# Strassen's seven products for the down projection of a fused attention and SwiGLU kernel, with casts moved from GpSimd to ScalarE

## The chip, the cores and the metric

The kernel runs on one core of a Trainium2 chip. The metric is the device time of one execution in microseconds. Before the change it took 389.86 us (median of 3 runs, 389.35 to 390.61). A run counts as slow when it takes over 1.5% longer than the fastest of the same kernel.

A word on names. PE is TensorE, DVE is VectorE, ACT is ScalarE, POOL is GpSimd, SP is SyncE. L634 is line 634 of that kernel's own source; the same statement has another line number in another kernel.

## The reference

Selective attention over 8 batches of 8 heads (sequence 576, head dimension 64), then a SwiGLU feed-forward block over all 4608 tokens, each with 512 features:

```python
scores = q @ k.T / sqrt(64)              # causal, plus min(bias, 0) from a cumulated s
attn   = exp(scores - max); attn /= attn.sum() + 1e-9
x      = (attn @ v) as (4608, 512)
g      = x @ w_gate                      # (512, 1536)
out    = (silu(g) * (x @ w_val)) @ w_out # w_out is (1536, 512), the "down projection"
```

Inputs and output are fp32; the kernel computes in bf16 with fp32 accumulation.

## The kernel before

After a start-up of about 32 us, in which batch 0 is attended, the kernel goes through nine **token tiles** of 512 tokens, numbered 0 to 8. Each has a **gate/value stage** (12 feature blocks of 128; for each a gate group and a value group of four 512-wide matmuls) and a **down stage** (four row groups of twelve 512-wide matmuls). The attention of the later batches is woven between the groups of tiles 0 to 5 and the start of tile 6: a generator yields after each group and the attention is pumped up to a given position. Every engine works through its own list in the order in which the program issues it. Eight PSUM banks are handed round by `take` and `give`.

```python
def ffn_items(tt):
    xt = XT[:, :, (tt % 3) * TT : (tt % 3 + 1) * TT]
    hts = []
    # ... the stores left over from the tile before are issued here
    for ft in range(NFT):                       # 12 feature blocks
        gbs = take(); pg = view(gbs, TT)
        for c in range(4):
            nc.tensor.matmul(pg, WG[j][:, c, f0:f0+128], xt[:, c, :], start=(c==0), stop=(c==3))
        nc.scalar.activation(th, pg, AF.Tanh, scale=0.5)
        nc.vector.scalar_tensor_tensor(pp, in0=th, scalar=1.0, in1=pg, op0=ALU.add, op1=ALU.mult)
        give(gbs)
        yield 1
        vbs = take(); pv = view(vbs, TT)
        # ... four matmuls with WV into pv
        ht = hpool.tile([128, TT], BF16, tag="ht", bufs=16, name="ht")
        nc.vector.tensor_mul(ht, pp, pv)
        give(vbs)
        hts.append(ht)
        yield 1
    for ts_ in range(4):                        # the down stage
        ybs = take(); py = view(ybs, DM)
        for ft in range(NFT):
            nc.tensor.matmul(py, hts[ft][:, ts_*128:(ts_+1)*128], WO[ft//WKO][:, ft%WKO, :],
                             start=(ft == 0), stop=(ft == NFT - 1))
            if ft % 4 == 3 and ft < NFT - 1:
                yield 1
        ysb = yp.tile([128, DM], FP32, tag="y", name="ysb")
        nc.scalar.mul(ysb, py, 0.5)
        give(ybs)
        # ... the store of the row group before is issued on GpSimd's queue
        yield 1
    # (the last row group of tile 8 goes in two halves of 256 columns, stored by SP)
```

What the attention does for the half-batch (four heads) that comes next stands beside this. SP loads fp32 keys and queries, they are cast to bf16 (`ck`, `cq`), written to memory (`ks`, `qs`), read back transposed (`pk`, `pq`), and copied by VectorE into the two halves of `kq`, from which PE takes the scores. GpSimd also casts the values (`rawv` to `vt`), masks the exponentials (`affine_select`), and issues the store of each finished pair of heads (`ot` to `xs`), which SP reads back transposed into `XT`.

```python
def side(h, step):                              # h: half-batch, step: head within it
    # ...
        if step == 0: transposes(h + 1); aug(h + 1, GP4)
        if step == 2: split(h + 1, "k", nc.vector)    # 2 copies pk -> kq, 64x1152 bf16
        if step == 3: split(h + 1, "q", nc.vector)    # 2 copies pq -> kq
    # ...
        if step == 1: cast_one(h + 2, "k", nc.gpsimd)
        if step == 2: cast_one(h + 2, "q", nc.gpsimd)
        if step == 3: scratch(h + 2)
    # ...  on odd h, V of the next batch: five casts on GpSimd, in steps 1, 2 and 3
```

The softmax here doesn't subtract the row's maximum and nothing guards it: scores larger than these inputs give would overflow.

## Time and profile before

| | before |
|---|---|
| time, median | 389.86 us |
| span in the profile | 388.6 us |
| PE busy | 371.3 us, 96% |
| tiles 2 to 5, each, first gate matmul to next tile's first | 40.4, 40.2, 40.2, 40.3 us |
| of which gate/value and down | 26.9 to 27.1 and 13.3 us |
| tiles 6, 7, 8 | 36.4, 31.8, 31.3 us |
| last matmul to end of span | 4.2 us |

The tile times are read off the timeline: where the first matmul with `wg` of a tile starts, and the first one with `wo`. As PE hardly stops in the middle of the kernel, they add up to the span. The end in the timeline (start, duration, engine, line, operation, output and inputs, count, and in brackets the idle time before it with what ended it):

```profile
382.80 1.58 PE L604 MATMUL bank<-wo,ht 128*128 128x256 bf16 x13
...
383.52 1.69 SPq L614 DMA_DIRECT2D out_dram<-yh  x2
384.42 0.42 DVE L613 TENSOR_SCALAR yh<-bank 128x256 f32<-128x256 f32 x1 [9.15 <-PE bank L604]
```

After PE's last matmul only one eviction of 256 columns and one small store remain.

### The profile page before, as it was taken

How to read it: one execution, taken by the hardware profiler on the slowest of the kernel's cores; microseconds unless marked ns; L12 is line 12 of the kernel's file. 1: busy time of each engine (PE TensorE's matmuls, PEld its weight loads, DVE VectorE, ACT ScalarE, POOL GpSimd, SP SyncE). 2: the span in 40 equal slices, each digit the busy share in tenths (PEclk: the TensorE clock that was granted, in tenths of full speed). 3: DMA queues.
4: the chain of work that ended last, by engine and by line, in shares of the span. 5: the costliest groups of instructions: out<-in, count | busy, mean ns of one | idle time of the engine just before them, and what ended most of it. 6: DMA issues, size and time to landing. Idle time of an engine off the chain costs nothing.

```text
span 388.6 us, 7949 instructions
## 1 busy us (share of the span) xinstructions
PE 371.3 (96%) x3006; PEld 206.2 (53%) x3006; DVE 239.8 (62%) x431; ACT 214.5 (55%) x411; POOL 192.3 (49%) x329
## 2 busy tenths in 40 slices
PE   3779999999999999999999999999999999999995
PEld 3565556655555555555555555555555544444443
DVE  7676777468653786369735884488347625733750
ACT  7686877567646565566556655565464513323321
POOL 7683368656695756566656666576342220011001
PEclk9999999999999999999999999999999999999999
DMA  7999999996859998996789757964231222002002
GB/s 245 196 244 261 197 264 257 303 254 165 158 153 269 287 221 220 211 267 153 184 215 288 122 178 142 293 159 98 61 113 35 32 73 69 3 27 81 2 12 97
DMA packets 100534, 64.18 MB, mean 165 GB/s; under 512 B 81888, under 2 KB 85824, under 8 KB 100496
## 3 DMA queue, kind: packets, MB, share of 16 engines
q1 hardware_dynamic: 90816, 45.36, 50.3%
q0 software_dynamic: 9680, 18.32, 18.2%
q8 instruction: 23, 0.38, 0.4%
q14 instruction: 15, 0.12, 0.1%
HBM read 37.90 MB, written 19.86 MB: 149 GB/s over the span
## 4 chain that ended last, share of the span: by engine, by line
PE 82%; DVE 6%; DMA 5%; issue 3%; ACT 2%; POOL 0%; DVEq 0%; ACTq 0%; SPq 0%; POOLq 0%
PE bank L571 21%; PE bank L620 21%; PE bank L586 20%; PE bank L367 9%; PE bank L405 6%; DMA pk<-ks 2%; PE wide L367 2%; DVE pp L578 2%; ACT pt L380 1%; DVE ht L591 1%; DVE kq L320 1%; DMA kq<-HL 1%; PE one L405 1%; DMA XT<-xs 1%; DMA s_sb<-in_s_dram 1%
## 5 line engine op out<-in xcount | busy, mean ns | idle before, releaser
L380 ACT ACTIVATE pt<-bank 128x512 bf16<-128x512 f32 x224 | 104.1, 504 | 40.3 <-PE bank L367 28.5
L578 DVE SCALAR_TENSOR_TENSOR pp<-th,bank 128x512 bf16<-128x512 bf16 x108 | 74.1, 686 | 69.8 <-ACT th L576 69.0
L571 PE MATMUL bank<-XT,wg 128*128 128x512 bf16 x432 | 111.0, 379 | 1.1 <-DMA XT<-xs 0.5
L586 PE MATMUL bank<-XT,wv 128*128 128x512 bf16 x432 | 110.9, 379 | 0.2 <-DVE pp L578 0.2
L576 ACT ACTIVATE th<-bank 128x512 bf16<-128x512 f32 x108 | 64.5, 597 | 78.2 <-PE bank L571 73.9
L620 PE MATMUL bank<-wo,ht 128*128 128x512 bf16 x420 | 102.4, 379 | 0.0
L591 DVE TENSOR_TENSOR ht<-pp,bank 128x512 bf16<-128x512 bf16 x108 | 74.0, 685 | 8.8
L367 PEld LDWEIGHTS <-kq 128*128 128x128 bf16 x576 | 46.5, 99 | 40.3 <-issue 6.1
L367 PE MATMUL bank<-kq 128*128 128x128 bf16 (+4 forms) x504 | 65.9, 240 | 0.7 <-DVE ht L591 0.5
L383 POOL TENSOR_SCALAR_AFFINE_SELECT pt<-pt 128x512 bf16<-128x512 bf16 x64 | 41.0, 640 | 34.3 <-ACT pt L380 33.7
L571 PEld LDWEIGHTS <-wg 128*128 128x128 bf16 x432 | 38.3, 98 | 36.6 <-issue 1.2
L586 PEld LDWEIGHTS <-wv 128*128 128x128 bf16 x432 | 38.4, 98 | 35.1 <-issue 1.1
L620 PEld LDWEIGHTS <-ht 128*128 128x128 bf16 x420 | 37.1, 98 | 34.4
L405 PEld LDWEIGHTS <-pt 128*128 128x128 bf16 x960 | 41.5, 98 | 20.7
L439 POOL DMA_DIRECT2D xs<-ot x24 | 21.9, 913 | 60.8 <-DVE ot L422 60.8
L634 POOL DMA_DIRECT2D out_dram<-ysb x35 | 19.7, 562 | 60.9 <-ACT ysb L628 60.9
L628 ACT ACTIVATE ysb<-bank 128x512 f32<-128x512 f32 x35 | 20.9, 597 | 40.9 <-PE bank L620 39.7
L405 PE MATMUL bank<-vt,pt 128*128 128x65 bf16 x840 | 42.8, 194 | 0.0
L190 POOL DMA_DIRECT2D kq<-HL x52 | 31.3, 602 | 2.0 <-PE bank L571 1.6
L421 DVE RECIPROCAL rc<-bank 128x5 f32<-128x5 f32 x56 | 10.6, 190 | 34.4 <-PE bank L405 34.4
L422 DVE TENSOR_TENSOR ot<-bank,rc 128x320 bf16<-128x320 f32 x56 | 27.5, 491 | 1.9
L388 POOL TENSOR_SCALAR_AFFINE_SELECT pt<-pt 128x64 bf16<-128x64 bf16 x64 | 16.4, 256 | 21.3 <-ACT pt L380 21.1
(68 smaller groups left out, 211.1 us busy)
## 6 DMA issues: line engine op xcount, KB each, us to landing
out_dram<-ysb POOLq DMA_DIRECT2D x35, 256.0 KB, 3.3
rawk<-in_k_dram SPq DMA_DIRECT2D x15, 576.0 KB
rawq<-in_q_dram SPq DMA_DIRECT2D x15, 576.0 KB
rawv<-in_v_dram SPq DMA_DIRECT2D x32, 256.0 KB
xs<-ot POOLq DMA_DIRECT2D x24, 160.0 KB, 3.9
ks<-ck SPq DMA_DIRECT2D x11, 288.0 KB
qs<-cq SPq DMA_DIRECT2D x11, 288.0 KB
wg<-in_moe_w_gate_dram POOLq DMA_DIRECT2D x2, 768.0 KB, 11.6
```

What stands on the lines that cost most here:

```text
L190: engs[hh].dma_start(KQ[hb % 2][r][r0 : r0 + 4, :, e * S : (e + 1) * S], HL[bh : bh + 1, :, :, :],)
L367: nc.tensor.matmul(sc[:, o : o + w], T[:, 1, e * S + 128 * tj : e * S + 128 * (tj + 1)], T[:, 0, e * S + lo : e * S + hi], start=True, sto ...
L380: nc.scalar.activation(pt[:, c0 : c0 + W], sc[:, 0:W], AF.Exp, scale=0.125)
L383: nc.gpsimd.affine_select(pt[:, 1088:1600], pt[:, 1088:1600], pattern=[[0, 4], [1, 128]], compare_op=ALU.is_ge, fill=zreg, base=0, channel ...
L405: nc.tensor.matmul(av[:, bi * (D + 1) : (bi + 1) * (D + 1)], pt[:, c0 : c0 + 128], VT[b % 2][:, tj, h, :], start=(tj == 0), stop=(tj == bi),)
L422: nc.vector.tensor_mul(ot[:, :, e * D : (e + 1) * D], av3[:, :, 0:D], rc[:, :, None].to_broadcast([128, NCH, D]),)
L571: nc.tensor.matmul(pg, WG[j][:, c, f0 : f0 + 128], xt[:, c, :], start=(c == 0), stop=(c == 3),)
L576: nc.scalar.activation(th, pg, AF.Tanh, scale=0.5)
L578: nc.vector.scalar_tensor_tensor(pp, in0=th, scalar=1.0, in1=pg, op0=ALU.add, op1=ALU.mult)
L586: nc.tensor.matmul(pv, WV[j][:, c, f0 : f0 + 128], xt[:, c, :], start=(c == 0), stop=(c == 3),)
L591: nc.vector.tensor_mul(ht, pp, pv)
L620: nc.tensor.matmul(py, hts[ft][:, ts_ * 128 : (ts_ + 1) * 128], WO[ft // WKO][:, ft % WKO, :], start=(ft == 0), stop=(ft == NFT - 1),)
```

## The change

The intent is to take matmul cycles away from the engine that bounds the kernel. Strassen's scheme forms a product of 2 x 2 blocks with seven block products in place of eight. Here the two feature blocks of a pair and the two token halves of a tile give the blocks of the left factor, and the same pair with the two halves of the output columns those of `w_out`. The price is sums of blocks. VectorE forms two adds for each pair in the gate/value stage (512 and 256 elements a row) and GpSimd one difference; sums of the weights are made once; and the outputs are combined from fp32 parts in the down stage. The products that need no sums come first. To make room on GpSimd, the casts of keys and queries go to ScalarE and the V casts are spread out. Tile 0 keeps the plain form.

```diff
-                    cast_one(h + 2, "k", nc.gpsimd)
+                    cast_one(h + 2, "k", nc.scalar)
...
-                    cast_one(h + 2, "q", nc.gpsimd)
+                    cast_one(h + 2, "q", nc.scalar)
...
+        V_AT = {(1, 0): 0, (1, 2): 1, (2, 0): 2, (2, 2): 3, (3, 0): 4}
...
-                ht = hpool.tile([128, TT], BF16, tag="ht", bufs=16, name="ht")
-                nc.vector.tensor_mul(ht, pp, pv)
+                hp = hps[-1]                       # one tile for two feature blocks
+                nc.vector.scalar_tensor_tensor(
+                    hp[:, 2 * k2 : 2 * k2 + 2, :]..., in0=pp, scalar=0.5, in1=pv, ...)
                 give(vbs)
+                if k2 == 1 and tt > 0:
+                    su = PTP[0].tile([128, 3, HT], BF16, tag="su", bufs=NP, name="su")
+                    nc.vector.tensor_add(su[:, 0:2, :], hp[:, 0:2, :], hp[:, 2:4, :])   # L633
+                    nc.vector.tensor_add(su[:, 2, :], hp[:, 0, :], hp[:, 3, :])         # L634
+                    (nc.vector if ft == NFT - 1 else nc.gpsimd).tensor_sub(             # L635
+                        hp[:, 1:3, :], hp[:, 1:4:2, :], hp[:, 0:3:2, :])
...
+        def down_seven(tt, hps, sus):     # 7 products x 2 row groups x 6 matmuls of 256
+            # P0, P1: two products without sums, all pairs but the last, then the last pair
+            #   s3 = copy (ScalarE); de[0] = s3 + P (VectorE)
+            # Q0, Q1: su[2] x WS[0]; then (difference) x WS[1];  de[1] = de[0] + Q (VectorE)
+            # for g in 0, 1:
+            #   P[g] += su[0] x W, su[1] x W;  y[1:3] = copy (ScalarE)
+            #   Q[g] += (difference) x WS[2];  y[0:4:3] = de + Q (VectorE), minus y[1:3] (GpSimd)
+            #   the stores: two of 256 KB a row group, issued one row group later
...
-            span = 36
+            span = 36 if tt == 0 else 34.5
```

Buffers shrink to make room: the exponentials' tiles (`pt`) from 8 to 5, the output tiles from 3 to 2. P0, P1, Q0 and Q1 hold four of the eight banks through the down stage.

## The prediction

> **What bounds the kernel now.** I read the engine summary first, then the table by stretches, the chain that ended last, the waits, and the single groups.
>
> From the page:
>
> ```profile
> span 388.6 us, 7949 instructions
> PE 371.3 (96%) x3006; PEld 206.2 (53%) x3006; DVE 239.8 (62%) x431; ACT 214.5 (55%) x411; POOL 192.3 (49%) x329
> PEclk9999999999999999999999999999999999999999
> ```
>
> TensorE works for 371.3 of 388.6 us at full clock. What that hides is the load of the others inside a stage, so I cut token tile 3 or 4 (steady state) into its gate/value stage and its down-projection stage, and took three whole tiles beside it. The columns are the stretch, its length, and PE, PEld, DVE, ACT, POOL busy:
>
> ```profile
> 204.60:231.60 27.00, 27.00 (x232) 14.96 (x229) 21.11 (x38) 16.22 (x33) 17.45 (x30) 1.00 0.79 181
> 231.60:244.90 13.30, 13.30 (x108) 7.23 (x107) 5.50 (x12) 7.30 (x16) 7.83 (x13) 1.00 0.88 191
> ...
> 354.00:374.00 20.00, 20.00 (x94) 9.09 (x93) 15.33 (x23) 7.16 (x12) 0.54 (x1) 1.00 0.04 14
> ...
> 164.30:204.50 40.20, 40.20 (x341) 22.16 (x337) 25.68 (x48) 23.47 (x48) 25.18 (x42) 1.00 0.87 207
> ```
>
> PE has no idle time at all here, so a matmul cycle removed is a cycle of time. But VectorE is already at 21.11 of 27.00 in gate/value (78%) and only 5.50 of 13.30 (41%) in the down stage. Its 62% is an average of two very different stages.
>
> The chain agrees: 82% of it is PE, and the down projection of the last two tiles stands in it bare:
>
> ```profile
> 342.91 10.36 PE bank L620 x48
> ...
> 373.99 7.77 PE bank L620 x36
> 381.76 2.63 PE bank L604 x24
> ```
>
> The waits show that nobody holds PE up for long now; ScalarE and VectorE wait for PE, not the reverse:
>
> ```profile
> ACT th L576 <- PE bank L571: 73.9, 92, 1.9
> DVE pp L578 <- ACT th L576: 69.0, 72, 10.6
> ...
> PE bank L571 <- DVE pp L578: 0.4, 2, 0.2
> ```
>
> **What the Trainium skill says.** "TensorE: Matmul & The Clock Gate", section "Back-to-back issue gap", gives N/2.4 + 2.5 ns warm: 215.8 ns for 512 columns, 109.2 for 256. The trace agrees: 10.36/48 = 0.2158 us and 2.63/24 = 0.1096 us, weight loads hidden in both. So half-width matmuls lose only about 1.5%. "VectorE: DVE Perf Modes", section "The perf-mode tier table", has a bf16 add from SBUF at 2 elements a cycle (1224 ns for 2048) and anything with PSUM at 1. With the fixed part that this leaves (about 155 ns) an SBUF add of 512 is some 0.42 us and of 256 some 0.29 (estimates from that page; the kernel before has no such add). The PSUM half of the statement is seen: 512/0.96 + 153 = 686 ns, the mean of the SCALAR_TENSOR_TENSOR. "SBUF — State Buffer", section "Who interferes with whom", says that a VectorE instruction with two SBUF inputs contends with a GpSimd instruction that reads SBUF, and that in 2-port modes one of the two blocks. The trace has something like it: one form of copy takes between 441 and 1634 ns:
>
> ```profile
> L278 DVE COPY kq<-pk x22: 442/496/1634, 83.7 to 277.3; 64x1152 bf16<-64x1152 bf16 x22
> L278 DVE COPY kq<-pq x22: 441/630/929, 88.3 to 282.0; 64x1152 bf16<-64x1152 bf16 x22
> ```
>
> "GPSIMD Engine Reference", section "Elementwise — side-by-side cycle accounting", has a two-input add of 2048 in 4497 ns, 2.2 ns an element; so I estimate 1.1 to 1.3 us for 512. No row here shows one.
>
> **The change part by part.**
>
> *Matmuls.* In tiles 1 to 8 a down projection of 48 matmuls of 512 columns becomes 7 products x 2 row groups x 6 = 84 of 256. Before: 48 x 0.2158 = 10.36 us. After: 84 x 0.1096 = 9.21. Saved 1.15 us a tile, **9.3 us over eight** (2.4%). This lies wholly on the path, since PE is 100% busy there. It is the whole gain; everything else is cost.
>
> *VectorE, gate/value stage.* The product instruction keeps its size and PSUM operand (0.69). New per pair of feature blocks: an add of 512 and one of 256, 0.42 + 0.29 = 0.71, six times = 4.2 us, and one difference of 512 at the end, 0.42. Attention is spread over 34.5 units in place of 36, so its VectorE work here grows by 4% of about 4.6, 0.2 us. Sum 21.1 + 4.2 + 0.4 + 0.2 = 25.9 busy. The stage on PE: 24 groups x 0.8636 = 20.7, and 24/34.5 of eight heads at 1.15 us (0.70 scores, 0.45 values, from the timeline) = 6.4, so 27.1 us. That is **96%**, before any stall at the shared port. If each of the 12 adds meets GpSimd as the copies above do (their mean is 640, 0.2 over the free 441) there are 1 to 2 us more, and then VectorE bounds this stage.
>
> *VectorE, down stage.* Four 256-wide adds from PSUM (about 0.42, as the 256-wide eviction L613) and two 512-wide (0.69): 3.1 us onto some 5, in a stage of 9.2 + 2.8 = 12 us. It fits. Whole tile: 25.7 + 4.6 + 3.1 = 33.4 of 39.1 us.
>
> *Weights.* Six sums in the down stage of tile 0 (768 elements: four at about 0.55, two with a scalar at about 0.95, 4.1 us), where VectorE has 9 of 19 us free: hidden. Four differences at the head of tile 1's gate stage, 2.2 us, where it has nothing free: part of it shows.
>
> *ScalarE.* Plus 22 casts of 1152: the 576-wide one takes 657, and 0.834 ns an element (1024 against 512 wide: 1024 and 597) gives 1.14 us, 25 us in all. Evictions: before 4 x 0.60 a tile, after 2 x 0.39 + 2 x 0.60, 0.4 less. A tile goes from 23.5 to about 27.6 of 39: hidden.
>
> *GpSimd.* Minus 22 casts of 1.15 = 25 us. Plus five differences a tile at 1.1 to 1.3 and two fp32 ones of 512 about the same, 8 us a tile against 4.6 removed: from 25.2 to about 29 of 39. Busy, in order, but what it feeds is needed microseconds later.
>
> *PSUM.* Four of eight banks are held through the down stage, where one was. Scores and values share the other four; they need about one bank a microsecond there, so a bank comes back after some 3 us, against 1 to 2 needed. Tight, not binding.
>
> *End.* Before, PE ends at 384.4 and the last store carries 128 KB after a 0.42 us eviction. After, a 512-wide add (0.69), then two 256 KB stores issued one after the other by SP (0.85 us each in the last rows). That is 0.3 + 0.8 and the larger transfer, less the half that was issued last before: about **1 us lost**.
>
> *Sum without stalls:* 389.9 - 9.3 + 1.0 = 381.6.
>
> **Stalls, my choice.** Gate and value banks are freed by VectorE. In a stage with 4.3 bank takes per pair of 2.27 us and eight banks, a bank returns after 3.3 us; the normal way from the start of its matmuls to its release is 0.86 + 0.1 + 0.6 + 0.05 + 0.69 = 2.3. So VectorE may fall back 1 us before PE stops. At 96% with bursts (two copies of 0.5 to 0.64, two adds, an attention output) it will. I take 0.4 us in each of tiles 2 to 6, 1 us in tile 1 (weight differences), 0.3 in tiles 7 and 8, where VectorE needs per pair 2 x 1.39 + 0.7 = 3.5 against PE's 3.46: 3.6 us. Less 0.5 for old PE gaps that may be closed by the new order. Predicted 384.7.
>
> **Rivals.** (1) *VectorE becomes the bound.* Shared-port stalls of 0.15 us on each add give 1.8 us a tile more, and six middle tiles each lose 1 to 1.5 us: total stalls 8 to 10 us, time 388 to 391. For it: 96% load and the copies' spread. Against: a third of what GpSimd reads there, the casts, is taken away, and its differences are issued right after the adds, when VectorE turns to instructions with one PSUM input. (2) *PE stays the bound and the sums hide*: 381 to 382. For it: not one PE wait in the middle tiles today, and VectorE's surplus can spill into the down stage, where the products without sums come first and give the last pair over 2 us. Against: the 1 us of bank slack. (3) *Four held banks or a ScalarE cast ahead of an exp stop PE in the down stage*: some 0.5 us a tile, 386. ScalarE's 70% speaks against.
>
> **Range and chances.** Rival 2 gives the low end, rival 1 the high one: 381 to 388.8. Faster by over 2% means under 382.1, so stalls under half a microsecond in total: 0.22. Slower by 2% would need 17 us of stalls: 0.03.
>
> **What the profile after should show.** Down matmuls 84 a tile at 0.11 spacing, PE's sum lower by about 9; the SBUF adds at 0.42 and 0.29 where free, longer where GpSimd reads; VectorE at over 90% in gate/value and under 70% in the down stage; PE waits on VectorE's pp and ht, absent today, of 3 to 4 us in all, mostly tile 1; the distance from PE's last matmul to the end about 1 us longer. I am wrong if PE's spacing at 256 columns with a new weight load each exceeds 0.12, if PE's idle time does not grow or grows by over 7 us, or if PE waits mainly on ScalarE or GpSimd.

## The result, and the profile after

The changed kernel takes **403.25 us** (median of 4 runs, 401.25 to 404.92) against 389.61 (4 runs, 388.55 to 390.61) of the kernel before beside it. The ratio is 1.0345, interval 1.0306 to 1.0383: it is 3.4% slower. A ratio here is taken over the fast runs of the two kernels, so it is not quite the ratio of the medians. The prediction was 384.7 us with a range of 381.0 to 388.8: wrong in sign, and far outside.

From the page of the changed kernel (the summary, then the engines with their number of instructions, then the chain that ended last):

```profile
span 401.8 us, 8788 instructions
...
PE 365.4 (91%) x3282; PEld 234.5 (58%) x3282; DVE 318.6 (79%) x593; ACT 231.4 (58%) x433; POOL 233.6 (58%) x361
...
PE 61%; DVE 20%; DMA 12%; issue 3%; ACT 3%; POOL 1%; DVEq 0%; ACTq 0%; SPq 0%
```

PE's share of the last chain fell from 82% to 61%; VectorE and DMA took it. The same cut by stages as before, for tile 4 (columns: stretch, length, PE, PEld, DVE, ACT, POOL busy with their counts, granted clock, DMA share, GB/s), gate/value then down, and then tile 8's gate/value:

```profile
215.90:245.50 29.60, 27.58 (x236) 15.19 (x233) 27.06 (x49) 18.37 (x37) 21.95 (x33) 1.00 0.72 201
245.50:257.40 11.90, 11.90 (x142) 10.62 (x141) 9.23 (x20) 8.35 (x17) 6.88 (x13) 1.00 0.70 141
364.80:385.50 20.70, 20.70 (x98) 9.39 (x96) 18.03 (x33) 7.32 (x13) 9.48 (x11) 1.00 0.14 51
```

The down stage went from 13.3 to 11.9 us, with PE busy all the time. The gate/value stage went from 26.9 to 29.6 us, and PE now stands still for 2.0 of it, with VectorE at 27.06 of 29.60. In tile 8, which has the same six pairs of sums but no attention, the stage takes 20.7 us as before, VectorE at 87%, and PE has no gap. So the sums do not cost wherever they stand; the loss is where they stand beside attention. Tile by tile:

| tile | 0 | 1 | 2 | 3 | 4 | 5 | 6 | 7 | 8 | last matmul to end |
|---|---|---|---|---|---|---|---|---|---|---|
| before, us | 48.1 | 43.7 | 40.4 | 40.2 | 40.2 | 40.3 | 36.4 | 31.8 | 31.3 | 4.2 |
| after, us | 47.8 | 49.8 | 43.8 | 42.4 | 41.5 | 41.0 | 35.2 | 31.1 | 30.1 | 6.9 |
| after, less (before - 1.15) | | 7.3 | 4.6 | 3.3 | 2.4 | 1.9 | 0.0 | 0.5 | -0.1 | |

The last row is what each tile lost against the saving of 1.15 us that the matmuls give: **19.5 us in tiles 1 to 5, half a microsecond in tiles 6 to 8** (in tile 7, where PE waits 1.1 us for a transfer of `XT`, against 0.5 before). Another 2.7 us are lost after the last matmul.

The costliest new groups (line, engine, operation, output and input, count, then busy us and mean ns of one, then idle time just before and what ended it):

```profile
L635 POOL TENSOR_TENSOR ht<-ht 128x512 bf16<-128x512 bf16 x40 | 46.5, 1162 | 55.9 <-DVE su L633 50.2 <-PE bank L372 3.9 <-PE bank L618 1.8
L634 DVE TENSOR_TENSOR su<-ht 128x256 bf16<-128x256 bf16 x48 | 28.4, 591 | 0.0
L633 DVE TENSOR_TENSOR su<-ht 128x512 bf16<-128x512 bf16 x48 | 22.8, 474 | 1.7
L281 DVE COPY kq<-pq 64x1152 bf16<-64x1152 bf16 x22 | 19.1, 869 | 0.3
L281 DVE COPY kq<-pk 64x1152 bf16<-64x1152 bf16 x22 | 13.2, 598 | 2.7 <-DMA pk<-ks 2.5
```

The add of 256 elements takes longer than the add of 512. The spread of the single instructions says why (minimum, median, maximum in ns, then first and last start):

```profile
L634 DVE TENSOR_TENSOR su<-ht x48: 277/284/3729, 88.5 to 387.4; 128x256 bf16<-128x256 bf16 x48
```

Most take 284 ns, one takes 3729. Above the free time lie 28.4 - 48 x 0.284 = 14.8 us for L634, 22.8 - 48 x 0.426 = 2.4 us for L633 (its median is 426), and the key and query copies, 28.1 us before by the two rows in the prediction, are now 32.3. That rise does not need the adds and differences, though: in the run without sums (below), which has neither, these copies take 32.8 us. Its query copies:

```profile
L281 DVE COPY kq<-pq 64x1152 bf16<-64x1152 bf16 x22 | 21.6, 982 | 0.4
```

There, the query copies overlap for 5.7 us with GpSimd's new fp32 subtractions of the outputs (`ysb`). By tiles 1 to 8, the excess of L634 is 2.4, 5.0, 1.9, 1.9, 1.9, 1.5, 0, 0 us: none in tiles 7 and 8, where GpSimd has no attention work.

The timeline at one such place, in tile 3; the same pattern comes back in tiles 2, 4 and 5 at 152.5, 236.5 and 277.5 us (rows of DVE, POOL and PE; others are left out):

```profile
194.96 0.71 DVE L633 TENSOR_TENSOR su<-ht 128x512 bf16<-128x512 bf16 x1
195.32 0.82 POOL L179 CAST vt<-rawv 64x512 bf16<-64x512 f32 x1
...
195.59 1.80 DVE L634 TENSOR_TENSOR su<-ht 128x256 bf16<-128x256 bf16 x1
...
196.11 1.14 POOL L635 TENSOR_TENSOR ht<-ht 128x512 bf16<-128x512 bf16 x1
...
197.32 0.97 DVE L281 COPY kq<-pq 64x1152 bf16<-64x1152 bf16 x2
...
197.86 0.38 PE L372 MATMUL bank<-kq 128*128 128x128 bf16 x4 [1.93 <-DVE kq L281]
```

Read it downwards; the profile's spans on GpSimd are rough. The last V cast of a batch runs on GpSimd from 195.32 to 196.14. VectorE's add L634 is up at 195.59, but does not end. When the cast ends, GpSimd's next instruction, the difference L635, runs at once, though the add had been there before it. L635 depends on the first add alone (its blocks 1 and 2 are read by L633, not by L634), so it lay ready behind the cast. Only after L635 ends, at 197.25, can the add finish, at 197.39. The query copies stand behind it in VectorE's list; PE needs them, and has waited 1.93 us. In tiles 4 and 5 this one stop (1.94 and 1.56 us) is the only one of PE over 0.1 us. Such stops make up the largest of PE's new waits:

```profile
PE bank L372 <- DVE kq L281: 8.8, 5, 1.9
...
PE bank L372 <- DVE pp L610: 2.4, 3, 1.1
```

The columns are the total in us, how often, and the longest. And the end of the changed kernel:

```profile
394.01 0.82 PE L671 MATMUL bank<-WS,ht 128*128 128x256 bf16 x6
...
394.88 0.72 DVE L717 TENSOR_TENSOR de<-de,ysb 128x512 f32<-128x512 f32 x1 [1.23 <-ACT ysb L714]
395.35 1.09 POOL L731 DMA_DIRECT2D out_dram<-ysb  x2 [0.30 <-POOL ysb L726]
395.78 0.69 DVE L721 TENSOR_TENSOR ysb<-de,bank 128x512 f32<-128x512 f32 x1 [0.19 <-DVE de L717]
396.54 0.83 SPq L731 DMA_DIRECT2D out_dram<-ysb  x2
```

VectorE has two instructions of 0.7 us in a row after PE's end, and four stores of 256 KB leave within 2 us, where the kernel before had one small one left.

### The profile page after: what moved, and what is told of

Read it like the earlier page. It is cut to its first block, busy times and chain, and to the rows that moved or that the text cites. A ratio compares the mean times of both kernels' runs of the same rounds, so it can differ in the third digit from the quotient of the medians.

```text
span 401.8 us, 8788 instructions
## 1 busy us (share of the span) xinstructions
PE 365.4 (91%) x3282; PEld 234.5 (58%) x3282; DVE 318.6 (79%) x593; ACT 231.4 (58%) x433; POOL 233.6 (58%) x361
## 4 chain that ended last, share of the span: by engine, by line
PE 61%; DVE 20%; DMA 12%; issue 3%; ACT 3%; POOL 1%; DVEq 0%; ACTq 0%; SPq 0%
PE bank L671 18%; PE bank L618 14%; PE bank L603 14%; DMA pk<-ks 8%; PE bank L372 5%; DVE ht L626 5%; PE bank L410 4%; DVE pp L610 4%; DVE su L634 3%; DVE kq L281 2%; DVE ot L427 2%; PE wide L372 2%; DVE su L633 2%; PE bank L647 2%; ACT pt L385 1%
## 5 line engine op out<-in xcount | busy, mean ns | idle before, releaser
L385 ACT ACTIVATE pt<-bank 128x512 bf16<-128x512 f32 x224 | 105.8, 507 | 42.5 <-PE bank L372 26.0
L626 DVE SCALAR_TENSOR_TENSOR ht<-pp,bank 128x512 bf16<-128x512 bf16 x108 | 74.0, 685 | 9.7
L372 PE MATMUL bank<-kq 128*128 128x128 bf16 (+4 forms) x504 | 68.1, 240 | 12.2 <-DVE kq L281 8.8
L635 POOL TENSOR_TENSOR ht<-ht 128x512 bf16<-128x512 bf16 x40 | 46.5, 1162 | 55.9 <-DVE su L633 50.2
L388 POOL TENSOR_SCALAR_AFFINE_SELECT pt<-pt 128x512 bf16<-128x512 bf16 x64 | 44.2, 690 | 24.8 <-ACT pt L385 24.3
L410 PEld LDWEIGHTS <-pt 128*128 128x128 bf16 x960 | 41.7, 98 | 17.3 <-issue 2.1
L671 PEld LDWEIGHTS <-ht 128*128 128x128 bf16 x384 | 35.5, 98 | 5.3 <-issue 0.3
L726 POOL TENSOR_TENSOR ysb<-ysb 128x512 f32<-128x512 f32 x15 | 18.9, 1263 | 26.4 <-DVE ysb L721 25.5
L671 PEld LDWEIGHTS <-su 128*128 128x128 bf16 x288 | 26.8, 98 | 3.7
L634 DVE TENSOR_TENSOR su<-ht 128x256 bf16<-128x256 bf16 x48 | 28.4, 591 | 0.0
```

The lines of the kernel that those rows point to most:

```text
L372: nc.tensor.matmul(sc[:, o : o + w], T[:, 1, e * S + 128 * tj : e * S + 128 * (tj + 1)], T[:, 0, e * S + lo : e * S + hi], start=True, sto ...
L385: nc.scalar.activation(pt[:, c0 : c0 + W], sc[:, 0:W], AF.Exp, scale=0.125)
L388: nc.gpsimd.affine_select(pt[:, 1088:1600], pt[:, 1088:1600], pattern=[[0, 4], [1, 128]], compare_op=ALU.is_ge, fill=zreg, base=0, channel ...
L410: nc.tensor.matmul(av[:, bi * (D + 1) : (bi + 1) * (D + 1)], pt[:, c0 : c0 + 128], VT[b % 2][:, tj, h, :], start=(tj == 0), stop=(tj == bi),)
L626: nc.vector.scalar_tensor_tensor(hp[:, 2 * k2 : 2 * k2 + 2, :].rearrange("p a n -> p (a n)"), in0=pp, scalar=0.5, in1=pv, op0=ALU.mult, op ...
L634: nc.vector.tensor_add(su[:, 2, :], hp[:, 0, :], hp[:, 3, :])
```

## The experiments

Theories, by the letters that the quoted texts use. **A**: the adds, having two SBUF inputs, are blocked by GpSimd at the shared port (the prediction says which rule is meant). **B**: VectorE's added working time is the bound, blocked or not. **C**: the loss comes from what the change does besides the sums (casts, buffers, order, transfers). **S**: the output stores, now two of 256 KB for each row group and issued in lumps, hold back the transposing reads of the keys. All times are medians; beside each stands the ratio to the kernel before on the same chip. The kernel before gave medians of 389.05 to 389.89.

### First: the order of the adds, no sums, the casts alone, the differences on VectorE

**The 256-wide add first.** The last add then reads the blocks that the difference overwrites, so GpSimd's difference cannot start ahead of it.

```diff
-                    nc.vector.tensor_add(su[:, 0:2, :], hp[:, 0:2, :], hp[:, 2:4, :])
                     nc.vector.tensor_add(su[:, 2, :], hp[:, 0, :], hp[:, 3, :])
+                    nc.vector.tensor_add(su[:, 0:2, :], hp[:, 0:2, :], hp[:, 2:4, :])
```

> The changed kernel with only the order of VectorE's two adds turned: the 256-wide one first, then the 512-wide one that the GpSimd difference waits for. Theory A (VectorE's SBUF adds stand still while GpSimd reads SBUF, and its own GpSimd difference takes the port again before the second add gets it): the mean of the 256-wide add falls from 591 ns to 400 or less, PE's idle time shrinks by 5 us or more, time 394 to 399. Theory B (VectorE simply has too much work in the gate/value stage, blocked or not): the same work, so 401 to 405 as the changed kernel.

Measured: 400.72 us, 1.0298 (1.0254 to 1.0341), correct. The blocking of the adds fell as A has it: the 256-wide one to a mean of 348 ns (free: 292) and the 512-wide one to 508 (free: 418), together 7 us of excess in place of 17. But the time fell by only 2.5 us by the medians, between the ranges of A and B; the two intervals of the ratios overlap, so the gain itself is hardly clear of noise. Tiles 4 and 5 gained nothing (41.5 and 41.1 us, against 41.5 and 41.0): in tile 4 the query copies now stand beside the difference and take 0.89 us each, and PE's stop of 1.94 us has become four of 0.24, 0.78, 0.59 and 0.18. Undoing this one order is not enough.

**No sums at all** (wrong results): the adds and the difference are left out, and the products read the unsummed blocks.

```diff
-                if k2 == 1 and tt > 0:
-                    su = ...
-                    nc.vector.tensor_add(...); nc.vector.tensor_add(...); (...).tensor_sub(...)
-                        lambda p: sus[p][:, 2, cols[g]], lambda p: WS[:, p, 0, :])
+                        lambda p: hps[p][:, 2, cols[g]], lambda p: WS[:, p, 0, :])
   ... and likewise sus[p][:, 0] -> hps[p][:, 0], sus[p][:, 1] -> hps[p][:, 1]
```

> Wrong result on purpose: the two adds and the difference of each pair left out, the products read the blocks themselves; all else as changed (products, casts on ScalarE, evictions, stores). A and B: PE bounds again, 389.6 - 9.3 for the matmuls + about 3 for the longer end = 382 to 385. Theory C (the products themselves, the four held banks or the ScalarE casts hold PE up): 390 or more.

Measured: 391.01 us, 1.0052 (1.0003 to 1.0102). The sums thus cost some 12 us (403.25 - 391.01). But even without them the kernel is not faster than before, although the 84 matmuls a tile are in: A and B both missed, and the time lies in the range given for C. In its profile tiles 5, 6 and 8 have their full saving, tile 4 loses 0.7 us against before, and one long stop stands out, in tile 2 (46.0 us):

```profile
142.18 0.92 DVE L281 COPY kq<-pk 64x1152 bf16<-64x1152 bf16 x2 [5.28 <-DMA pk<-ks]
...
143.87 1.87 PE L618 MATMUL bank<-XT,wv 128*128 128x512 bf16 x4 [3.83 <-DVE ht L626]
```

VectorE waits 5.28 us, in its fixed order, for a transposed key block to arrive; the banks behind it are not freed, and PE stops for 3.83 us. So there is a second limit, in the transfers.

**The casts alone**, on the kernel before:

```diff
-                    cast_one(h + 2, "k", nc.gpsimd)
+                    cast_one(h + 2, "k", nc.scalar)
   ... the same for q, and the V casts at the five places of the change
```

> The kernel before with only the casts moved (k, q casts of half-batches 5 to 15 on ScalarE, V casts spread). A and B: PE still bounds, 388.5 to 391, and the kq copies on VectorE get nearer their free 442 ns (mean was 640), since GpSimd reads less. Theory D (casts on ScalarE delay exps and with them PE): 393 or more.

Measured: 389.17 us, 0.999 (0.9956 to 1.0025), correct. Moving the casts costs nothing and gains nothing; the query copies did not get nearer to their free time either (mean 662 ns). This part of C falls.

**All differences on VectorE**, so that GpSimd has none of the new SBUF reads in the gate/value stage:

```diff
-                    (nc.vector if ft == NFT - 1 else nc.gpsimd).tensor_sub(
+                    nc.vector.tensor_sub(
```

> The changed kernel with all six differences of a tile on VectorE in place of five on GpSimd: VectorE has 5 x 0.42 = 2.1 us a tile more, GpSimd 46 us less, so blocked adds are rarer. A: what is saved in blocking (17 us over the kernel) is about what is added (17 us): 398 to 404. B: 2 us a tile more in a stage that is bound by VectorE, seven tiles: 413 to 420.

Measured: 402.30 us, 1.0323 (1.027 to 1.0376), correct. GpSimd's 46.5 us of differences become some 18 on VectorE (21.9 in all, 3.5 of which were there before), and nothing is won. The three sums there have means of 416 ns (free: 284), 514 (426) and 455 (418): they still meet the casts and masks of GpSimd. The differences belong on neither engine in these tiles.

### Second: the stores, V casts on ScalarE, the weights, the end

**No sums, stores later.** The two row groups' stores go into the next tile's gate/value stage, at its feature blocks 7 and 9, in place of the head of the tile. Its output is wrong, which doesn't matter for the time.

```diff
+                if ft in (7, 9) and stores:
+                    stores.pop(0)()
...
-                flush()
...
-            flush()
             yield from gate_value(tt, hps, sus)
```

> Wrong result on purpose: the run without sums, and the two 512 KB stores of a tile issued in the middle of the next tile's gate/value stage (blocks 7 and 9) in place of together at its start. Theory S (1 MB of stores in one lump delays the transposing loads of k that tile 2 to 4 wait for): the 5.3 us wait of VectorE for pk in tile 2 halves or goes, PE's 3.8 us stop there with it, time 384 to 387. Theory L (the loads of k, q, v alone keep the DMA engines full there): 390 to 392 as before.

Measured: 387.99 us, 0.9938 (0.9883 to 0.9993), 3 us below the run with early stores. It is 1 us above S's range, but clearly below L's, and the stop in tile 2 shrank (40.5 us in place of 46.0). So S holds: without the sums, the lump of stores was the next limit. The whole of the matmuls' saving is still not there (9.3 us); VectorE waits 13.0 us for transposed keys, and the end costs 2.8.

**V casts on ScalarE** too, with the adds swapped as in the first run, so that little on GpSimd reads SBUF:

```diff
-                cast_v(bn, V_AT[step, ci], nc.gpsimd)
+                cast_v(bn, V_AT[step, ci], nc.scalar)
```

> The changed kernel with the adds in turned order and the V casts on ScalarE in place of GpSimd. Theory A (shared port) says that what remains of blocking in the gate/value stage comes from these casts and the masks: the 256-wide adds reach 0.30 us, PE waits 1 to 2 us less in each of tiles 1 to 5 than in the turned run, 392 to 397. B (VectorE's own work): within 1.5 us of the turned run's 400.7.

Measured: 404.72 us, 1.0374 (1.031 to 1.0438), correct. The adds are nearly free (means 338 and 457 ns). But tile 0 takes 55.0 us in place of 47.8, because ScalarE waits up to 5.8 us in its order for a load of V, while tiles 1 to 5 take 214.1 us together, 1.8 less than with the swap alone (215.9). The experiment hurt something else, so its total proves nothing; its tiles 1 to 5 suggest that the last bit of blocking of the adds was a small part of what remained.

**No weight differences** (wrong): the four instructions at the head of tile 1 are left out.

```diff
-            todo = {0: W_SUMS, 1: W_DIFFS}.get(tt, [])
+            todo = {0: W_SUMS}.get(tt, [])
```

> Wrong result on purpose: the four weight differences at the head of tile 1 left out (2.2 to 2.6 us of VectorE). If tile 1's long period (49.8 against 43.7 before) is theirs, it falls to about 46.5 and the kernel to about 400; if it is the adds and copies alone, less than 1 us.

Measured: 402.95 us, 1.0339 (1.0276 to 1.0402). Tile 1 falls from 49.8 to 47.0, and tile 2 gives half of it back (43.8 to 45.2): part of what is taken away at one place shows up at the next.

**Order of the end**: in tile 8, row group 0 is finished before row group 1 is begun.

```diff
+            order = (q_part, 0), (q_part, 1), (p_part, 0), (p_part, 1)
+            if tt == NTT - 1:
+                order = (q_part, 0), (p_part, 0), (q_part, 1), (p_part, 1)
```

> The changed kernel, in the last tile alone the first row group finished before the second's sums (Q0, P0, Q1, P1 in place of Q0, Q1, P0, P1), so that half the last megabyte leaves about 2.6 us earlier. If the end is long because four 256 KB stores leave together, the distance from PE's last matmul to the end of the span falls from 7.0 to about 5.3 us; if it is the chain of copy, subtract, add and issue, it stays at 6.5 to 7. Total 401 to 403.

Measured: 402.27 us, 1.0321 (1.0266 to 1.0375), correct. From PE's last matmul to the end it is 5.5 us in place of 6.9. The order is worth about 1.4 us of the 2.7.

### Third: VectorE's load without the shared port; the key and query copies elsewhere

**The decisive one: load without port.** On the run without sums and with late stores, VectorE gets per pair of feature blocks one dummy instruction of 512 columns that reads PSUM, so it has one PSUM input and no second SBUF input. Wrong results.

```diff
+                if k2 == 1 and tt > 0:
+                    dm = PTP[0].tile([128, TT], FP32, tag="su", bufs=2, name="dm")
+                    nc.vector.tensor_scalar_mul(dm, pv, 0.5)
                 give(vbs)
```

> Wrong result on purpose: no sums, late stores, and in each pair of tiles 1 to 8 one VectorE instruction that reads 512 columns of PSUM and writes SBUF (about 0.69 us, as long as both adds unblocked[...]). Theory B: the load alone is enough, gate/value stages of tiles 1 to 5 as long as with sums in the turned order (29 to 30 us), 395 to 398. Theory A: without blocking the load hides, 388 to 390 as the run without it.

Measured: 389.64 us, 0.9987 (0.994 to 1.0035). The group has 48 instructions of 684 ns, 32.8 us, against 48 x (0.426 + 0.284) = 34.1 us for the two adds when free; so it is almost the same load, in the same place. It even holds a bank longer. In its tile 4, gate/value (columns as above):

```profile
206.50:233.70 27.20, 27.20 (x238) 15.12 (x235) 24.50 (x45) 18.35 (x37) 17.75 (x32) 1.00 0.77 215
```

VectorE is 90% busy, and PE has no gap at all: 27.2 us, where the prediction worked out 27.1 for a stage with attention moved up. The load as such hides there. Theory B falls, up to this load. It is not free everywhere: tiles 1 and 2 take 46.1 and 41.4 us, against 44.0 and 40.5 without it, and some stops of PE end with the dummy instruction. It ran in 683 to 687 ns every time, so it was not blocked itself.

**Swapped adds with late stores** (the two mends together, correct results):

```diff
   adds in the order of the first run, and
+                if ft in (7, 9) and stores:
+                    stores.pop(0)()
```

> The changed kernel with the adds in turned order and the stores of a tile issued in the middle of the next one's gate/value stage. Late stores were worth 3 us without sums. If that gain and the turned order's 2.5 us add, 397 to 399; if VectorE's work now hides the DMA (it reaches the copies later anyway), 400 to 401.

Measured: 405.04 us, 1.0393 (1.0353 to 1.0432). Late stores gain 3 us without the sums and lose 4.3 us with them. The query copies take 1187 ns on average, their highest yet. I had not expected the sign, and why it is so was not found.

**Key copies, then key and query copies, on ScalarE**, on top of all the mends:

```diff
-                    split(h + 1, "k", nc.vector)
+                    split(h + 1, "k", nc.scalar)
   ... and in the second kernel also
-                    split(h + 1, "q", nc.vector)
+                    split(h + 1, "q", nc.scalar)
```

> As the run before, with the 22 copies of transposed k into kq on ScalarE (about 1.1 us each there) in place of VectorE, and the last tile's end in the new order. Theory B (VectorE's work bounds the gate/value stage): half of the copies gone, 1 us a tile in the gate/value stages of tiles 1 to 5, 391 to 395. Theory A (blocking by GpSimd alone): these copies blocked little (0.59 against 0.44), so 396 to 398.

> As the run before, with q's copies on ScalarE as well. B: VectorE falls below 90% in the gate/value stage, PE bounds tiles 2 to 8: 384 to 390. Rival: ScalarE, now at over 70%, delays tanh and exp and takes VectorE's place as the bound: 392 or more, with PE waits named after ScalarE.

Measured: 415.94 us, 1.0689 (1.0653 to 1.0724), and 417.03 us, 1.0631 (1.0572 to 1.0691), both correct. Of the second's four runs two were slow (418.82, 418.68); the fast ones took 415.38 and 412.19, and the ratio is of these. No range was met but that of the rival, 392 or more. PE then waits for the exponentials, 13.2 us in five waits with both moved, up to 4.9 at once: ScalarE works in order too, and a copy that waits for its transfer holds the next exponential. That is no way out.

### Fourth: adds and differences apart

On the run without sums and with late stores: the differences alone (as in the change, on GpSimd), the adds alone (swapped), and the dummy load with the differences. Their outputs are wrong, which doesn't matter for the times.

```diff
   differences alone, after give(vbs):
+                if k2 == 1 and tt > 0:
+                    (nc.vector if ft == NFT - 1 else nc.gpsimd).tensor_sub(hp[:, 1:3, :], ...)
   adds alone, at the same place, with the products reading su again:
+                    nc.vector.tensor_add(su[:, 2, :], hp[:, 0, :], hp[:, 3, :])
+                    nc.vector.tensor_add(su[:, 0:2, :], hp[:, 0:2, :], hp[:, 2:4, :])
   dummy load and differences: the dm instruction of above, and the tensor_sub
```

> Wrong result on purpose: the run without sums and with late stores (388.0), plus only the differences (five of six a tile on GpSimd, 1.16 us each). If GpSimd's differences alone cost the time (they hold the shared port against the kq copies, and delay the masks behind them): 394 or more. If they matter only together with VectorE's adds: 388 to 390.

> Wrong result on purpose: both adds on VectorE in the turned order, late stores, no differences at all. If the adds' own wait for the port counts (masks and V casts stay): 394 to 400, and the adds at about 0.45 us on average. If the differences are needed for the loss: within 2 us of the equal load from PSUM, 388 to 391.5.

> Wrong result on purpose: the equal load from PSUM in the place of the adds (389.6), plus the differences on GpSimd. Nothing of VectorE's new work can be blocked now; only the kq copies can. If load and differences together make the loss: 398 or more, near the 405.0 of turned adds with late stores. If the adds' need of the port is essential: 390 to 393.

With the runs that share their base, each as a median less that of the kernel before:

| on the base with late stores | median, us | over before, us | ratio |
|---|---|---|---|
| no sums | 387.99 | -1.1 | 0.9938 |
| VectorE load from PSUM | 389.64 | +0.5 | 0.9987 |
| differences on GpSimd alone | 395.51 | +5.6 | 1.0140 (1.0099 to 1.0180) |
| load and differences | 395.53 | +5.6 | 1.0184 (1.0131 to 1.0238) |
| adds on VectorE alone | 394.31 | +4.4 | 1.0119 (1.0089 to 1.0149) |
| adds and differences | 405.04 | +15.9 | 1.0393 |

Against the first row: load 1.5 us, differences 6.7, adds 5.5, adds and differences 16.9, which is 4.8 more than the two by themselves. By the ratios that excess is only 2.8 us, and the intervals of the four ratios together leave about 3 us of doubt, so it is not shown that the pair costs more than its parts. Load on top of the differences adds nothing by the medians, and 0.4% by the ratios, whose intervals overlap (the verdict of that run against the kernel before is unclear, and its time lies between its two ranges). So what is done with the time is what counts: an equal load from PSUM costs 1.5, the adds 5.5. Why the adds alone are not free: GpSimd's casts and masks read SBUF as well, and their means were 394 and 502 ns, 8.9 us above the free 292 and 418. Why the differences alone cost 6.7 us is shown only in part: GpSimd is busy for 232.2 us in place of 186.6, and VectorE waits longer for keys. Total, times and longest of that wait, with the differences alone:

```profile
DVE kq L281 <- DMA pk<-ks: 17.1, 8, 3.5
```

It was 13.0 us without them, and the query copies went from 1016 to 1115 ns. But with load and differences, at the same total, that wait is 5.5 us, so it does not account for the loss.

**Sevens only where attention is over**, in tiles 6 to 8 (adds swapped, the end reordered, the casts of keys and queries left on GpSimd, and half of the last output finished early):

```diff
+        T0 = 6
-                if k2 == 1 and tt > 0:
+                if k2 == 1 and tt >= T0:
-            if tt == 0:
+            if tt < T0:
                 yield from down_plain(tt, hps)
-            span = 36 if tt == 0 else 34.5
+            span = 36 if tt < T0 else 34.5
```

> Seven products only in tiles 6, 7 and 8, where attention is over or nearly so and the changed kernel kept its whole gain; tiles 0 to 5 and all casts as in the kernel before; adds in turned order; in the last tile the first row group first, and the half of the last store that does not need the last product sent ahead. Each of the three tiles gains about 1 us (1.2, 0.7 and 1.2 in the changed kernel), the end should lose at most 0.5 to 1.5: 386.5 to 388.5, and correct.

Measured: 392.82 us, 1.0084 (1.0059 to 1.0109), correct, so a miss by over 4 us. Two faults of mine are in the profile. These are a wait of PE, then one of ScalarE (total, times, longest):

```profile
PE bank L672 <- DVE ysb L720: 2.0, 1, 2.0
```

```profile
ACT ysb L656 <- DMA out_dram<-ysb: 12.8, 5, 3.1
```

PE's last product waits 2.0 us for VectorE to read half of the same bank; and with two output tiles in place of three, ScalarE's evictions in the plain tiles wait for stores, 12.8 us in all, so tiles 3 to 5 take 41.1 to 41.2 us in place of 40.2.

### Last: the two faults mended, and one tile more

The last product goes into a fresh bank, the plain tiles use both halves of the output tiles (four slots), and the casts go to ScalarE as in the change. The second kernel starts the sevens at tile 5.

```diff
+                if ts_ % 2 == 0:
+                    ysb = yp.tile([128, 2, DM], FP32, tag="y", name="ysb")
+                nc.scalar.copy(ysb[:, ts_ % 2, :], py)
...
+                    RB = take()
+                    R = view(RB, HD)
-                product(Q[g][:, 0:HD], False, True,
+                product(R if end else Q[g][:, 0:HD], end, True,
   ... and in the second kernel
-        T0 = 6
+        T0 = 5
```

> Seven products only in tiles 6 to 8, where the changed kernel kept its full gain, with the two faults of the run before it (sevens 6 to 8) mended: the last product of tile 8 writes a fresh bank, so TensorE does not wait for an eviction, and the plain tiles have four output slots instead of two. My theory (the sums cost only where they meet GpSimd's key, query and value work, in tiles 1 to 5): tiles 1 to 5 at 43.0, 40.5, 40.2, 40.2, 40.3 us as with the casts alone, tiles 6 to 8 at 35.2, 31.1, 30.0, that is 3.3 us less than before; tail after TensorE's last matmul 3.5 to 4.5 us. Time 385.5 to 387.5 us, ratio 0.990 to 0.996. If the sums cost wherever they stand, or the tail eats the gain: 389 or more.

> The same with the seven products from tile 5 on. In the changed kernel tile 5 took 41.0 us against 40.3 before: its down stage gained 1.3 and its gate and value stage lost 2.0. My theory: tile 5 loses what it gains, so 385.5 to 388.5 us, no better than sevens from tile 6. If the losses of tiles 1 to 5 are only a lateness handed on from tile 1, which a kernel that starts the sums in tile 5 has not got, tile 5 takes 39.1 and the time is 1.2 us below that of sevens from tile 6.

Measured: from tile 6, **388.35 us**, 0.9978 (0.9957 to 0.9998); from tile 5, 390.10 us, 1.0004 (0.9982 to 1.0027); both correct, 5 rounds. Tile by tile:

| tile | 1 | 2 | 3 | 4 | 5 | 6 | 7 | 8 | last matmul to end |
|---|---|---|---|---|---|---|---|---|---|
| casts alone | 43.0 | 40.5 | 40.2 | 40.2 | 40.3 | 36.4 | 32.0 | 31.3 | 3.9 |
| sevens from 6 | 42.4 | 40.6 | 40.2 | 40.2 | 40.3 | 35.8 | 31.0 | 29.8 | 5.4 |
| sevens from 5 | 42.4 | 42.0 | 40.2 | 40.2 | 42.2 | 35.2 | 31.1 | 29.8 | 5.4 |

From tile 6, tiles 6 to 8 save 3.0 us against the casts alone, near the 3.3 expected; but the end costs 5.4 us and not the 3.5 to 4.5 that I had expected, as three VectorE instructions stand in a row there:

```profile
380.28 0.69 DVE L720 TENSOR_TENSOR de<-de,ysb 128x512 f32<-128x512 f32 x1 [1.55 <-ACT ysb L717]
381.06 0.69 DVE L721 TENSOR_TENSOR ysb<-de,bank 128x512 f32<-128x512 f32 x1
...
381.85 0.42 DVE L734 TENSOR_TENSOR ysb<-ysb,bank 128x256 f32<-128x256 f32 x1
```

PE ended at 380.2. It is the only version with correct results whose interval leaves out 1 on the faster side, and that barely: 0.2%, about 1 us. It missed my range of 385.5 to 387.5 by 0.85 us. From tile 5, the one tile loses what it should gain and more: 42.2 us against 40.3 plain and the 39.1 that a pure saving would give. Nothing late was handed on to it, since tiles 3 and 4 ran at 40.2. So a lateness handed on from tile 1 is not needed for a loss. But this tile is not tile 5 of the changed kernel, for I overlooked that the four weight differences move with the start. Here they stand in tile 5, with 3.3 us of VectorE (lines as in the table of groups):

```profile
L593 DVE TENSOR_TENSOR wo<-wo 128x768 bf16<-128x768 bf16 x2 | 1.9, 933 | 0.0
...
L589 DVE TENSOR_TENSOR wo<-wo 128x768 bf16<-128x768 bf16 x2 | 1.5, 731 | 0.0
```

PE's first stop in the tile ends at 259.50, 2.7 us after the end of the last of them, and in tile 1 of the changed kernel their removal took off 2.8 us. How much of the loss is theirs and how much that of the sums was not separated. (Tile 2 of that kernel took 1.4 us more than in its pair, with the same plain code; VectorE waited 2.58 us for a key block there, in the pair 1.17. That is part of the difference of 1.75 us between the two medians.)

## Why the prediction was wrong, point by point

**The matmuls: right.** 84 matmuls of 256 took 9.17 us in the chain of the changed kernel against the 9.21 worked out, so 10.36 - 9.17 = 1.19 us a tile. (The section "Back-to-back issue gap" of the Trainium skill's "TensorE: Matmul & The Clock Gate" gives the formula used here for an isolated matmul; for a sustained stream it has about 131 ns at 512 columns. The streams of this kernel show 215.8 ns.) The down stages fell by 1.2 to 1.5 us, and tiles 6 to 8 together by 3.1. The sum of PE's busy time fell by only 5.9 us in the changed kernel (371.3 to 365.4), though by 9.2 without the sums and with late stores (362.1); where the sums put stops into PE's stream its recorded busy time is longer. What that is was not settled.

**VectorE's load: about right, and not the cause.** 96% busy in gate/value was worked out. A measured 90% without the adds, tile 4 of the dummy load, hides completely (27.2 us, no gap). In the down stage "under 70%" was forecast, and tile 4 shows 9.23 of 11.90 us, 78%, at no cost to PE.

**The step that failed** is this one: "I take 0.4 us in each of tiles 2 to 6, 1 us in tile 1 (weight differences), 0.3 in tiles 7 and 8". It is the term of the sum for stalls, 3.6 us. Measured against the same saving it was 7.3, 4.6, 3.3, 2.4 and 1.9 us in tiles 1 to 5, and half a microsecond in tiles 6 to 8. It was too small by a factor of more than five, and it had the places wrong: stalls were given to tiles 6 to 8 for VectorE's load there, but tile 8 has 87% load and no stop of PE, and the one in tile 7 is for a transfer. The 7.3 of tile 1 is not the weight differences alone: without them it became 4.5, and tile 2 took 1.4 more. The path was wrong as well: the waits on `pp` and `ht`, through the banks, were forecast at 3 to 4 us and measured about 4.5 (1.3 before); the largest, 8.8 us on the copies into `kq`, is not in the prediction. A late VectorE stopped PE above all through the copy that stood next in its list. The prediction's own sign of being wrong came up: PE's idle time grew by 19 us (17.3 to 36.4), not by under 7. The slack of 1 us that the term rests on does not follow from its numbers either: eight banks at 4.3 takes in 2.27 us give 4.2 us until a bank comes back, not 3.3.

**Why it failed.** The working names the mechanism ("If each of the 12 adds meets GpSimd as the copies above do ... there are 1 to 2 us more") and then leaves it out of the central sum. Its own numbers, 12 adds at 0.2 us, give 2.4 us, and the adds' excess in tiles 3 to 5 was 2.3 to 2.7 us a tile; as a term of the sum it would have been right there. The ground for leaving it out was that GpSimd's differences "are issued right after the adds, when VectorE turns to instructions with one PSUM input". That is the order of issue in the program. What GpSimd waits for is the data, and the difference needs only the first add. It therefore ran ahead of the second one. The rule of the shared port was cited correctly; what was not worked out is which instruction is ready first on the other engine. But this order is a small part of the loss at most: swapping the adds (400.72) took off 2.5 us by the medians, and nothing in tiles 4 and 5.

**The rivals.** Rival 1 had the right direction and cause (stalls at the shared port, 1.8 us a tile) and gave 388 to 391. It came short by 12 us. What it did not count are the differences (6.7 us by themselves) and the end (2.7 in place of 1). Rival 2 (the sums hide) is true of tiles 6 to 8 only. Rival 3 fell in the form given: the down stages have no PE gap but one of 0.25 us in tile 1, so four held banks suffice, and the casts on ScalarE are harmless.

**The end: direction right, size wrong.** 1 us was predicted, 2.7 measured. Left out was that VectorE has two fp32 instructions in a row, 0.72 and 0.69 us, where the plain form has one of 0.42.

**The transfers: missed.** The prediction has no term for DMA. Even with no sums the kernel is no faster than before (391.01) until the stores are moved (387.99), where key transposes that come late hold VectorE's list (5.28 us at once in tile 2).

**What stays open.** The 17 us of adds and differences are shown to be tied to tiles 1 to 5 and not to VectorE's working time. For the adds the contention with GpSimd is seen (8.9 us over their free time when they stand alone, 5.5 us of loss); for the differences the path is not shown. How they divide into adds blocked, copies blocked, and transfers that start late since GpSimd issues them late, was not separated: no mend of the changed kernel (swap, late stores, V casts on ScalarE, no weight differences) took off more than 2.5 us, and some moved the wait to another place. That the GpSimd lateness runs through the stores of `xs`, SP's ordered list and the key transposes is argued, not shown, and the waits speak for it only weakly: SP's wait for `xs` is 86.8 us without sums and 93.6 with the differences, but 93.4 with the adds alone and 93.9 without sums and with early stores; it is 110.5 in the changed kernel.

## What to carry to other kernels

When a bound engine is relieved by work on two others, first ask whether these two share a port, and for each pair of instructions which is *ready* first, by data and not by the order in which the program lists them. An estimate that names a contention and leaves it out of its sum is a choice; take the measured spread of a similar instruction (here 441 to 1634 ns) as a term, for all that queues behind it too. Use the trick where its helpers are idle: the seven products paid in tiles 6 to 8, where attention is over or nearly so.

## What the Trainium skill lacked or had wrong

- "SBUF — State Buffer", "Who interferes with whom": it says that the one that issues first holds the shared pair for its whole instruction and that the other blocks until then. The runs show that a VectorE add, once blocked, can also wait for the next GpSimd instruction that lies ready. The 256-wide add that is up at 195.59 ended after the cast *and* after a difference that started 0.52 us later: 1.80 us for 0.28. The longest of 48 took 3.73 us. The page has no word on who gets the port next among those that wait.
- "GPSIMD Engine Reference", "Elementwise — side-by-side cycle accounting": its two-input figure, for 2048 elements of fp32, scales to 512 as estimated (1.1 to 1.3 us): the 512-wide fp32 subtraction took 1.263 us on average. It lacks bf16, where the difference took 1.153 us (median), little less.
- No page that I found has a figure for what it costs when in-order engines wait on each other's late transfers; here 5.28 us of VectorE waiting for one transposed key block became a stop of PE of 3.83 us.
